# Sixteen places later for the first expert's transposes in attention's order of steps

## The chip, the cores and the metric

The kernel runs on one core of one Trainium2 chip. The metric is the device time of one execution in microseconds. An attention layer is followed by two mixture-of-experts layers, all in one launch.

## The reference

```python
def _attn_ref(q, k, v):                    # (4, 12, 448, 64), float32
    scores = (1 / sqrt(64)) * q @ k.T      # per batch and head, 448 x 448
    attn = softmax(causal(scores))
    return attn @ v

def _moe_ref(x, modality_id, w_gate, modality_bias, w1, w2):   # x: 1792 tokens x 768
    logits = x @ w_gate + modality_bias[modality_id]           # 8 experts
    e_idx = np.argmax(logits, axis=1)
    gate_w = softmax(logits)[token, e_idx]
    for e in range(8):
        h = np.maximum(x[mask] @ w1[e], 0.0)                   # 768 -> 1024
        out[mask] = gate_w[mask, None] * (h @ w2[e])           # 1024 -> 768

def reference(q, k, v, ...):
    x = attn_out.transpose(0, 2, 1, 3).reshape(1792, 768)
    return _moe2_ref(_moe_ref(x, ...), ...)                    # two such layers, the second without a bias
```

## The kernel before, in words

**Attention** works on 24 pairs of heads, numbered 0 to 23 (4 batches of 6). The work on a pair is cut into some fifty small steps, named in `ORDER`: `trans` (transposes of q and k on TensorE), `thi` and `tlo` (their high parts on ScalarE, their low parts on VectorE), `mv` (copies inside the on-chip memory, issued on SP), `score` (TensorE, L165 and L166), `mini` (mask and minimum on VectorE, L171), `expo` (ScalarE, L178, writes P), `ptrans` (TensorE, L194), `phi` and `plo` (ScalarE L201, VectorE L207), `pv` (TensorE, L214 and L215), `ocopy` (ScalarE, L220), `ria` (GpSimd, L224), `ri` (VectorE, L227), `final` (TensorE, L235), `norm` (VectorE, L244 and L246) and `store` (issued on SP, L251). A number behind the name is the head of the pair and the row block. `ORDER` is written out by hand and is run once per body; its colon number says how many pairs behind the body a step works. The text writes `norm_0@20` for that step on pair 20. Every engine, and SP, takes its instructions in the order in which the program lists them. The score banks are three, taken in turn: one of attention's own and the two banks (h0, h1) that the first expert's matmuls use later.

**Other work is hung into that order.** `ORDER` holds 24 entries `step` in each body. At each of them one entry of a list `todo` is run, and at every fifth one entry of a list `slow`. After a batch of pairs is stored, `batch` (b = 0 to 2) fills `todo` with the routing of that batch. For b = 2 the list ends with work on the **first block of the first expert** of the first expert layer, the block with which that layer begins: a gather of 128 token rows from memory into `xg` (L795, issued on GpSimd), then `XW` empty entries (`r1.wait`), then for each half g of the rows the transposes `xput` (three on TensorE, L806, into `m1xt`), `xhigh` (ScalarE, L809, into `xh`) and `xlow` (VectorE, L813, into `xl`), and last four loads that bring that expert's w2 into `raw` (L754, issued on SP, 768 KB each). `slow` brings w1 and splits it: its high parts are `high` (ScalarE, L765, some 1.05 us each), the first three low parts run on GpSimd (L769).

When no score step is left and `slow` and `todo` are both empty, each `step` runs one entry of a third list, `drain`: the first matmuls of that expert's block, `up0`, two matmuls for each of 12 pairs of column half and slice (L832 and L833, from `xh`, `xl` and the high part of w1). What is left after the last body runs behind it. Then `block0` (L851 among others) finishes the block; its second product reads w2 straight from `raw`.

```python
fs += [r1.wait, lambda: m1.gather(r1.slo[:, ds(e0["dve"] * MB, 1)], x1[: (B - 1) * S, :])] + [r1.wait] * XW
for g in range(2):
    fs += [r1.opens(lambda g=g: xput(g)), lambda g=g: m1.xhigh(t[g], g), r1.closes(lambda g=g: m1.xlow(t[g], g))]
fs += [lambda i=i: e0["second"][i]() for i in range(KF // 2)]
...
if at > free and drain and not hooks["slow"] and not todo:
    drain.pop(0)()
```

An entry marked `opens` takes a bank of the two that `trans` and `final` also use; `room` lets it run only if no more than two are held until the entry marked `closes`.

Of the kernel before, what the change touches and what calls it, by code (L numbers as in the profile page):

```python
# [324 lines left out]
            f()  # L325


PW, PL, XW = 12, 4, 8
HA, HB = 5, 5
WS, FILL = 8, 10  # L330
ET = mybir.EngineType
# [1111 lines left out]
```

## Time and profile before

| | |
|---|---|
| median of 3 runs | 960.15 us (960.14 to 960.53) |
| the profiled execution | 961.24 us |
| its span, first to last instruction | 959.3 us |
| TensorE busy in it | 913.3 us (95%) |
| VectorE, ScalarE, GpSimd busy | 627.3, 494.3, 170.8 us |
| mean granted TensorE clock | 0.984 |

The span is what the trace shows; the profiled execution is 1.94 us longer than it, and 1.09 us above the median of the runs. Times in the rows below count from the span's start, in microseconds. Attention takes the first 272 us or so, and the change stands at its end.

### The profile page before, as it was taken

The page shows a single profiled execution, that of the slowest core. Times are in us where ns is not written, and L with a number is a line of the kernel's source. Part 1 is how long each engine was busy: PE and PEld are TensorE (multiplying, and loading weights), DVE is VectorE, ACT ScalarE, POOL GpSimd, SP SyncE. Part 2 cuts the span into 40 slices and gives each one's busy share as a digit, 9 for nine tenths or more (in the row PEclk, how much of TensorE's full clock was granted, in tenths as well). Part 3 has the DMA queues.
Part 4 walks back from the last instruction along what each step waited for, and adds up shares of the span by engine and source line. Part 5 has one row for each costly group of instructions (what it writes and reads, how often), then busy time and mean ns, then how long its engine had stood idle before and what let it go on. Part 6 is the DMA issues. An engine that isn't in the chain of part 4 may idle for free. (4 is left out here: it accounts for less than half of the span.)

```text
span 959.3 us, 21195 instructions
## 1 busy us (share of the span) xinstructions
PE 913.3 (95%) x5432; PEld 808.9 (84%) x5433; DVE 627.3 (65%) x1792; ACT 494.3 (52%) x1137; POOL 170.8 (18%) x225
## 2 busy tenths in 40 slices
PE   8999999996999999997999899999999999999996
PEld 5998898986877889887898788689888888988895
DVE  4999999997574776798766778521177117383743
ACT  4998888886652222262222167322276227483653
POOL 5122414227320000000000000110112102131202
PEclk7999999999999999998999999999999999999999
DMA  6777887877249211137121135351159116395610
GB/s 124 170 185 174 185 204 186 178 165 195 95 138 343 82 49 54 64 127 251 49 66 49 45 115 200 134 212 42 40 183 357 77 46 217 105 352 221 240 49 8
DMA packets 121721, 138.50 MB, mean 144 GB/s; under 512 B 77175, under 2 KB 96759, under 8 KB 121350
## 3 DMA queue, kind: packets, MB, share of 16 engines
q1 hardware_dynamic: 116902, 118.23, 40.5%
q0 software_dynamic: 4768, 19.67, 6.0%
q8 instruction: 22, 0.36, 0.2%
q14 instruction: 29, 0.24, 0.1%
HBM read 117.69 MB, written 24.01 MB: 148 GB/s over the span
## 5 line engine op out<-in xcount | busy, mean ns | idle before, releaser
L769 DVE TENSOR_TENSOR l<-raw,h 128x768 fp32r<-128x768 f32 (+1 forms) x148 | 147.5, 1059 | 13.0 <-ACT h L765 12.7
L765 ACT CAST h<-raw 128x768 fp32r<-128x768 f32 (+1 forms) x154 | 131.3, 926 | 7.7 <-issue 5.7
L866 DVE SCALAR_TENSOR_TENSOR htl<-m2ht,hth 128x512 fp32r<-128x512 f32 x36 | 24.8, 689 | 142.7 <-ACT hth L865 142.7
L1253 DVE CUSTOM_DVE_ANT_0 junk<-y,wgb 128x768 bf16<-128x768 f32 x104 | 99.5, 956 | 14.2 <-ACTq L900 8.6
L178 ACT ACTIVATE P<-ps,m 112x336 f32<-112x336 f32 (+1 forms) x192 | 95.6, 508 | 20.5 <-DVE m L171 19.8
L844 PE MATMUL m2y<-h,hth 128*128 128x384 f32 x272 | 93.1, 342 | 0.0
L171 DVE CUSTOM_DVE_ANT_0 ps<-ps,mask 112x336 f32<-112x336 f32 (+1 forms) x192 | 85.5, 454 | 11.3 <-PE ps L163 4.6
L844 PE MATMUL m2y<-h,htl 128*128 128x384 f32 x272 | 91.5, 337 | 0.0
L832 PE MATMUL m2h<-h,xh 128*128 128x512 f32 x204 | 81.9, 401 | 1.2 <-ACTq L947 1.2
L207 DVE TENSOR_TENSOR ptl<-pp,pth 112x448 fp32r<-112x448 f32 x144 | 77.6, 539 | 8.2 <-ACT pth L201 8.1
L833 PE MATMUL m2h<-h,xl 128*128 128x512 f32 x204 | 80.9, 397 | 0.0
L194 PE MATMUL pp<-cident,P 112*112 112x112 f32 x480 | 72.5, 265 | 5.0 <-DVE ptl L207 4.5
L201 ACT CAST pth<-pp 112x448 fp32r<-112x448 f32 x144 | 67.2, 481 | 17.4 <-PE pp L194 16.7
L844 PE MATMUL m1y<-h,htl 128*128 128x384 f32 x192 | 65.9, 343 | 5.3 <-DVE htl L866 5.3
L844 PE MATMUL m1y<-h,hth 128*128 128x384 f32 x192 | 67.7, 353 | 0.0
L194 PEld LDWEIGHTS pp<-cident,P 112*112 112x112 f32 x480 | 52.8, 136 | 14.6 <-PE ps L166 5.0
L795 POOL DMA_INDIRECT xg<-y_scratch,ic x21 | 21.4, 1020 | 232.9 <-PE m2y L844 148.3
L214 PE MATMUL po<-pth,vs 112*128 112x448 f32 x192 | 62.4, 338 | 0.0
L165 PE MATMUL ps<-xk,xq 128*112 128x336 f32 (+3 forms) x184 | 61.0, 339 | 1.4 <-DMA xq<-ql 0.7
L844 PE MATMUL m2y<-l,hth 128*128 128x384 f32 x272 | 60.2, 342 | 1.1 <-issue 0.4
L795 POOL DMA_INDIRECT xg<-x_scratch,ic x16 | 16.4, 1026 | 248.3 <-PE m1y L844 223.2
L1189 POOL DMA_INDIRECT out_dram<-y,ic x19 | 36.4, 1918 | 124.2 <-ACTq L900 66.0
(459 smaller groups left out, 2202.7 us busy)
## 6 DMA issues: line engine op xcount, KB each, us to landing
raw<-in_moe_w_dram SPq DMA_DIRECT2D x46, 1536.0 KB, 10.3
xk<-xk SPq DMA_DIRECT2D x69, 112.0 KB, 3.5
y_scratch<-y SPq DMA_DIRECT2D x16, 384.0 KB
lk<-in_k_dram SPq DMA_DIRECT2D x48, 112.0 KB, 2.7
lq<-in_q_dram SPq DMA_DIRECT2D x48, 112.0 KB, 3.0
lv<-in_v_dram SPq DMA_DIRECT2D x24, 224.0 KB, 4.5
x_scratch<-xs SPq DMA_DIRECT2D x24, 224.0 KB, 3.2
xq<-ql SPq DMA_DIRECT2D x46, 112.0 KB, 3.0
```

Of the source, the lines that this page charges most:

```text
L171: nc.vector.tensor_tensor_reduce(out=s["ps", i], in0=s["ps", i], in1=mask[:, S - (i + 1) * CP :], scale=1.0, scalar=3.0e38, op0=ALU.add, o ...
L178: nc.scalar.activation(P, s["ps", i], AF.Exp, bias=s["m"][:, i : i + 1], scale=-1.0, accum_out=rs[:, j, i : i + 1])
L194: nc.tensor.transpose(pt[:, at : at + CP], s["P", i][:, kc * CP : (kc + 1) * CP], ident[:CP, :CP])
L201: nc.scalar.copy(h[:, a : a + w], pt)
L207: nc.vector.tensor_tensor(out=l[:, a : a + w], in0=pt, in1=s["pth"][:, a : a + w], op=ALU.subtract)
L214: nc.tensor.matmul(o[:, kc * CP :], vs[:, j, kc, :], s["pth"][:, seg], start=kc == 0, stop=False)
L765: self.nc.scalar.copy(hi[k], raw[:, k, :])
L769: eng.tensor_tensor(out=lo[k], in0=raw[:, k, :], in1=hi[k], op=ALU.subtract)
L832: mm(ph, xh[:, s], W.h1[k][:, f], start=k == 0, stop=False)
L833: mm(ph, xl[:, s], W.h1[k][:, f], start=False, stop=False)
L844: mm(py[n], rows[p[0]][:, s], (W.h2 if p[1] == "h" else W.l2)[k][:, f], start=k == 0 and p == "hh", stop=stop and k == ks[-1] and p == par ...
L1253: vec.tensor_tensor_reduce(out=junk, in0=y, in1=wgb[:, e], scale=1.0, scalar=0.0, op0=ALU.mult, op1=ALU.add, accum_out=r2.lg[:, e : e + 1])
```

## The change

```diff
-PW, PL, XW = 12, 4, 8
+PW, PL, XW = 12, 4, 24
```

`XW` is used in one place, the list quoted above. Between the gather and the first `xput` stand 24 empty entries instead of 8. The two groups of `xput`, `xhigh` and `xlow` and the four loads of w2, ten entries in all, move 16 entries `step` later; the gather stays. No instruction is added or taken away.

Counted along `ORDER` (the entries `step` are numbered through from the first body): the gather stands at step 641 in both. The ten entries stand at steps 650 to 659 before and 666 to 675 after. `drain` starts at step 681 in both, because the last score step lies between 680 and 681.

## Rows read from the trace of the kernel before

**Rows 1.** Page, part 1: TensorE's busy time, share and instructions (the other engines follow).
```profile
PE 913.3 (95%) x5432; PEld 808.9 (84%) x5433; DVE 627.3 (65%) x1792; ACT 494.3 (52%) x1137; POOL 170.8 (18%) x225
```
**Rows 2.** Windows: stretch, length, busy PE PEld DVE ACT POOL, clock, DMA share, GB/s.
```profile
232.95:238.72 5.77, 0.00 (x0) 0.00 (x0) 1.83 (x8) 1.40 (x6) 5.11 (x5) 0.80 0.90 293
238.72:243.30 4.58, 4.54 (x24) 4.51 (x25) 1.38 (x4) 1.35 (x4) 0.00 (x0) 0.51 1.03 366
243.30:247.70 4.40, 4.23 (x29) 3.43 (x27) 2.75 (x11) 4.12 (x10) 0.00 (x0) 1.00 0.55 174
247.70:252.00 4.30, 2.99 (x24) 2.62 (x25) 3.24 (x12) 4.30 (x14) 2.13 (x3) 1.00 0.02 4
252.00:255.00 3.00, 3.00 (x27) 2.77 (x26) 2.89 (x11) 2.98 (x11) 0.00 (x0) 1.00 0.01 3
255.00:260.00 5.00, 5.00 (x28) 4.20 (x28) 1.82 (x6) 1.74 (x5) 1.25 (x2) 1.00 0.18 46
```
**Rows 3.** Waits of PE, 229 to 275: total us, times, longest.
```profile
PE m1xt L806 <- DMA xg<-x_scratch,ic: 5.8, 1, 5.8
```
**Rows 4.** Timeline at the gather: start, length, engine, line, operation, [idle before <-releaser].
```profile
232.35 1.28 POOL L795 DMA_INDIRECT xg<-x_scratch,ic  x1 [0.19 <-DVE ql L119]
...
232.77 1.08 SPq L754 DMA_DIRECT2D raw<-in_moe_w_dram  x2
...
238.75 0.87 PE L806 MATMUL m1xt<-cident,xg 128*128 128x128 f32 x3 [5.81 <-DMA xg<-x_scratch,ic]
```
**Rows 5.** Tile xg, 225 to 245, issue to landing; the page's median of 16 such gathers.
```profile
DMA to landing us min/median/max: 6.3/6.3/6.3
...
xg<-x_scratch,ic POOLq DMA_INDIRECT x16, 3.9
```
**Rows 6.** Timeline, ScalarE from the second xhigh on, and the first up0.
```profile
243.59 0.48 ACT L809 CAST xh<-m1xt 128x384 fp32r<-128x384 f32 x1 [1.26 <-PE m1xt L806]
...
251.29 0.28 ACT L178 ACTIVATION_READ_ACCUMULATOR P<-ps,m 112x1 f32 x1
...
252.41 0.45 ACT L178 ACTIVATE P<-ps,m 112x112 f32<-112x112 f32 x1
...
254.60 0.20 ACT L178 ACTIVATION_READ_ACCUMULATOR P<-ps,m 112x1 f32 x1
...
254.86 0.19 PEld L832 LDWEIGHTS m1h0a<-h,xh 128*128 128x128 f32 x1 [0.18 <-ACT P L178]
```
**Rows 7.** Timeline, VectorE: the first xlow, then plo_1_0@22 and the end of mini_0_0@23.
```profile
241.92 0.56 DVE L813 TENSOR_TENSOR xl<-m1xt,xh 128x384 fp32r<-128x384 f32 x1 [7.08 <-ACT xh L809]
...
250.83 0.62 DVE L207 TENSOR_TENSOR ptl<-pp,pth 112x448 fp32r<-112x448 f32 x1 [0.61 <-ACT pth L201]
...
251.56 0.14 DVE L171 DVE_READ_ACCUMULATOR2_ANT m<- 112x1 f32 x1
```
**Rows 8.** Timeline: ria@21 on GpSimd, and ri@21, which reads it, on VectorE.
```profile
238.00 0.24 POOL L224 TENSOR_SCALAR ri<-rs 112x8 f32<-112x8 f32 x1
...
244.87 0.19 DVE L227 RECIPROCAL ri<-ri 112x8 f32<-112x8 f32 x1
```
**Rows 9.** Timeline, SP: store@20, then store@22 and store@23 (merged, the last at 271.69).
```profile
243.79 0.34 SPq L251 DMA_DIRECT2D x_scratch<-xs  x1
...
266.45 5.24 SPq L251 DMA_DIRECT2D x_scratch<-xs  x2
```
**Rows 10.** Windows: the first stretch of 2 us without w2's transfer.
```profile
246.00:248.00 2.00, 1.66 (x10) 1.25 (x9) 0.63 (x3) 2.00 (x5) 0.24 (x1) 1.00 0.00 1
```
**Rows 11.** Timeline, TensorE: the first readers of w2's first and second half.
```profile
274.70 2.85 PE L851 MATMUL m1y0a<-raw,wgb 128*128 128x384 f32 x8
...
280.36 2.80 PE L851 MATMUL m1y0a<-raw,wgb 128*128 128x384 f32 x8
```
**Rows 12.** Timeline, TensorE: two up0 matmuls of one kind, one entry of drain apart.
```profile
256.29 0.39 PE L832 MATMUL m1h0a<-h,xh 128*128 128x512 f32 x1
...
256.76 0.39 PE L832 MATMUL m1h0a<-h,xh 128*128 128x512 f32 x1
```

## The prediction

> **What bounds the kernel now.** I first read the busy shares: TensorE is busy for 95% of the span [rows 1], so time comes back only where TensorE stands still or runs slowly. Then I read the waits of TensorE over the end of attention. One stands far above the rest: 5.8 us at the first `xput`, which waits for the gather of the token rows [rows 3]. The timeline shows why. GpSimd issues the gather at 232.35. TensorE has emptied its queue by 232.95 and stands before the transposes until 238.75 [rows 2, 4]. The gather takes 6.3 us from issue to landing [rows 5], and the loads of w2 go out on SP 0.4 us after it [rows 4], so both transfers share the DMA engines. In the table of stretches the reader should see three things [rows 2]: no TensorE work at all in 232.95 to 238.72; a granted clock of 0.51 in the 4.58 us behind that wait, which is the lower level of 1.2 GHz, and 1.00 (2.4 GHz) afterwards; and, from 243.30 to 255, ScalarE busy for 11.40 of 11.70 us, while TensorE drops to 2.99 of 4.30 us in the middle. From 255 on TensorE is busy all the time and the others are not. So there are three limits one behind the other: a DMA wait, then ScalarE, then TensorE.
>
> **What the change moves.** Nothing is added or removed. Ten entries go from steps 650 to 659 to steps 666 to 675: six transposes, two `xhigh`, two `xlow`, four issues of w2 on SP. The second `xput` now comes just ahead of the step `expo_1_1@23`, whose work ends at 251.57 today [rows 6]. Less the 7.9 us worked out below that is about 243.7, 11 us behind the gather's issue at 232.35; the first `xput` stands some 2 us ahead of it (an estimate: three steps at about 0.6 us). Both are later than the 6.3 us of the landing, so the gather is there.
>
> The stall itself: 5.8 us of waiting goes, and 4.54 us of TensorE work at half clock becomes about 2.3 us. Ceiling: 5.8 + 2.3 = 8.1 us. At the new place I find no TensorE wait of more than about 1 us in today's trace, and there the clock is 1.00 [rows 2], so I give the clock no new loss.
>
> What is late next: I add up the busy time of each engine over the five stretches from 232.95 to 255 [rows 2], since all of that work remains to be done. ScalarE: 1.40 + 1.35 + 4.12 + 4.30 + 2.98 = 14.15 us. VectorE: 1.83 + 1.38 + 2.75 + 3.24 + 2.89 = 12.09. TensorE, with the slow stretch halved: 2.27 + 4.23 + 2.99 + 3.00 = 12.5. So of 22.05 us no more than 22.05 - 14.15 = **7.9 us** can come back, because ScalarE has its work to do, the two moved `xhigh` (0.48 each) among it.
>
> What ScalarE loses beside that. The TensorE-bound tail begins with the first `up0`. It takes score bank h0, and it waits until ScalarE has read the scores of `expo_0_2@23`, which ends at 254.80 [rows 6]. The end of this `expo` decides the gain. Two frictions are before it:
> - About 0.2 us early on, where ScalarE waits for one `mini` and for one `ptrans` that TensorE can do only after 232.95 (an estimate from the order of the steps).
> - The second moved group. `xlow` of g = 1 now stands ahead of `plo_1_0@22` and `mini_0_0@23` in VectorE's queue, and it needs the `xhigh` that stands behind `expo_1_1@23` on ScalarE. On today's axis that `expo` ends at 251.57 [rows 6]; with the first `xhigh` ahead (about 0.4) it is 251.98, and the second `xhigh` ends at 252.46. VectorE then does `xlow` 0.56, `plo` 0.62 and the `mini` of 112 columns, about 0.41 [rows 7]: 254.05. ScalarE is ready for `expo_0_0@23` at today's 252.41 plus two `xhigh` of about 0.43 each, 253.27 [rows 6]. It waits 0.8 us. Today VectorE starts that `plo` at 250.83 and ends the `mini` at 251.70, 0.7 us ahead of ScalarE [rows 6, 7], so the slack was there and is used up.
>
> Sum: 7.9 - 0.2 - 0.8 = 6.9; I take **6.8 us** for the little that such handovers add. Its ends: 7.9 with no friction (8.1, the ceiling, if the busy sum hides overlap on ScalarE), and 4.8 if both groups show their whole chain, twice transposes 0.5 + `xhigh` 0.48 + `xlow` 0.56 = 3.1 us off 7.9. The value lies nearer to the upper end because the first group meets VectorE before it has anything that ScalarE waits for.
>
> GpSimd's queue: between the gather and `ria@21` it runs one low part of w1 and `splitv`, and `ria@21` ends at 238.24 whatever TensorE does [rows 8]. Today VectorE comes to `ri@21` at 244.87, long after. In the new order it would come there at about 237.0 (244.87 less the 7.9), so it waits some 1.2 us. Behind it stands `mini_1_3@22`, and ScalarE has two slices of w1 and two `phi` to do meanwhile, so I cost this at nothing; if that cover is gone it is 1.2 us.
>
> SP's queue: the four issues of w2 pass `mv_k_3@23`, `mv_q_3@23` and `store@20`, and come to stand right behind `store@20`, ahead of `store@21`. `store@20` waits for `norm_0@20`; it goes out at 243.79 today [rows 9], and about 7.5 us sooner, at some 236.3, once the stall is gone. So w2 starts at about 237 to 239 instead of 232.8. Today its transfer runs from 232.77 to before 246 [rows 4, 10], 13.2 us at most; then it ends by about 252. Its first reader stands at 274.70, about 267.9 on the new axis [rows 11]. Cover: 16 us. Cost nothing. The `mv` copies get the DMA engines to themselves for these 4 us, which I count as nothing too, since no score step waits for them.
>
> The Trainium skill, "DMA: Bandwidth & Descriptors", section "Rules for kernel authors", speaks against this half of the change: a transfer that is to lie beside computing should be issued early and waited for late. Here the issue becomes some 4 us later; by the rows the 16 us of cover pay for that, and by the rule it would count only if the cover were gone, which is the last rival below.
>
> The drain: the last of the ten entries runs at step 675, six before `drain` starts at 681, so `up0` keeps its place and only its `xh` and `xl` come later; they are there by step 671.
>
> **The number.** The profiled execution takes 961.24 us; less 6.8 it is 954.4. It lies 1.09 us above the median of the runs, so for the median I predict 960.15 - 6.8 = **953.3 us**, 0.7% less. A measurement of this kernel can tell about 0.2% (1.9 us) from no change.
>
> **The rivals.**
> - *Half of it is given back in the tight stretch.* Both groups show their chain (4.8 us are left), and the wait at `ri@21` isn't covered either (1.2): gain 3.6, **956.5 us**. For it: ScalarE is busy 4.30 of 4.30 us exactly where the groups go [rows 2]. Against it: VectorE is busy only 3.24 of these.
> - *The change doesn't do what it says, because the list runs too long.* If `room` refuses the banks for six steps or more, or the count is off, `drain` starts late and `up0` falls behind attention. Its 12 entries take 0.47 us each [rows 12], 5.6 in all, and would no longer fill the gaps of the tail: gain 6.8 - 5.6 = 1.2, **959.0 us**, no difference. Against it: at steps 666 and 669 no `trans` is left and the next `final` comes at 672, so a bank is free.
> - *Slower: w2 comes too late.* SP is in order, and w2 now stands behind a store. If SP held it until the last store, 271.69 - 6.8 = 264.9 [rows 9], its first half would land 6.6 us later at 271.5, against a need at 267.9: 3.6 us of waiting (13.2 us for the whole, so 6.6 for a half); the second half, at 278.1 against 273.6 + 3.6 = 277.2, adds 0.9 [rows 11]. TensorE would then run at the low clock, as behind today's stall, 2.3 us: 6.8 together, no gain. The gather of the next block falls beside this transfer and would take today's 6.3 us instead of the median 3.9 [rows 5]: 2.4 more, and the kernel ends slower, at **962.6 us**. The point from which it decides is a landing of the first half some 4 us behind 268; the plan's order puts it at about 246 (237 to 239 and half a transfer).
>
> **How the numbers follow.** Forecast (gain 4.8 to 8.1, 952.0 to 955.4) 0.72; half given back 0.14; list too long 0.07; w2 late 0.05; 0.02 for no reason that I can name, as no change. The range holds forecast and first rival, from 951.9 (ceiling and 0.1 of scatter) to 956.6. Faster by over 0.2% (below 958.2): 0.72 + 0.14 + some of the third case, 0.87. Within 0.2%: 0.08. Slower by over 0.2% (above 962.1): 0.05.
>
> **What would show it.** In the changed kernel's waits of TensorE the 5.8 us line at `m1xt` is gone or under 0.5 us, and no stretch between 232 and 262 is at a clock under 0.9. The first `up0` starts at about 248.0 instead of 254.86, and everything behind it is earlier by the same amount. VectorE waits at `ri` for GpSimd near 238.2. ScalarE waits for `mini_0_0@23` for some 0.8 us. SP issues w2 between 236 and 240, and the first L851 waits for nothing. I am wrong if the stall comes up again elsewhere (at L851, or at a `final` that waits for a bank), or if the first `up0` is earlier but the end isn't.

## The result and the profile after

| | before | after |
|---|---|---|
| median of the runs beside each other | 960.33 us (4 runs, 960.14 to 960.53) | 953.03 us (4 runs, 951.76 to 953.51) |
| ratio, 95% interval | | 0.9918 (0.9891 to 0.9944) |
| beside the runs further down | 961.63 us (23 runs) | 953.97 us (6 runs), 0.9917 (0.989 to 0.9945) |
| profiled execution, its span | 961.24, 959.3 us | 953.22, 950.1 us |

The kernel became 7.3 us faster, against 6.8 forecast. The span fell by 9.2 us, more than the median; the first lines show why. They are the two timelines' twelve warm-up matmuls at the start of the program, of before and then of after, both long ahead of the change:

```profile
1.50 5.30 PE L267 MATMUL warm<-mask 112*128 112x512 bf16 x12 [1.50 <-DVE mask L259]
```

```profile
1.50 4.45 PE L267 MATMUL warm<-mask 112*128 112x512 bf16 x12 [1.50 <-DVE mask L259]
```

The same instructions take 0.85 us less, and by the gather's issue the execution after is 1.86 us ahead (230.49 against 232.35). None of this is the change, which stands behind the gather: in the traces of the runs below that have the same work ahead of the gather, its issue lies between 230.5 and 233.2. So I compare distances from the gather's issue. Timeline of after, the end of attention (columns as in [rows 4]):

```profile
230.49 1.28 POOL L795 DMA_INDIRECT xg<-x_scratch,ic  x1 [0.17 <-issue]
...
231.46 0.55 SPq L139 DMA_DIRECT2D xq<-ql  x1
...
234.29 0.32 SPq L251 DMA_DIRECT2D x_scratch<-xs  x1
...
234.81 3.16 SPq L754 DMA_DIRECT2D raw<-in_moe_w_dram  x4
...
236.47 0.20 DVE L227 RECIPROCAL ri<-ri 112x8 f32<-112x8 f32 x1 [1.82 <-POOL ri L224]
...
237.01 0.49 PE L806 MATMUL m1xt<-cident,xg 128*128 128x128 f32 x3
...
243.28 0.35 ACT L178 ACTIVATE P<-ps,m 112x112 f32<-112x112 f32 x1 [0.34 <-DVE m L171]
...
245.91 0.19 PEld L832 LDWEIGHTS m1h0a<-h,xh 128*128 128x128 f32 x1 [0.45 <-ACT P L178]
```

From the gather's issue to the first `up0` it is 15.4 us; before it was 22.5 (254.86 - 232.35, [rows 4, 6]). That is 7.1 us. The transposes come 6.5 us behind the gather's issue and wait for nothing. From there on nothing is gained or lost: from the first `up0` to the first matmul of the next block, `m1h0f`, it is 33.3 us in both, and from that to the end of the span 671.1 and 670.9. Windows of after (columns as in [rows 2]):

```profile
232.00:236.00 4.00, 3.99 (x33) 3.52 (x32) 2.60 (x9) 3.90 (x13) 3.92 (x3) 1.00 0.82 205
236.00:240.00 4.00, 2.94 (x21) 2.31 (x21) 2.68 (x11) 4.00 (x10) 2.48 (x5) 1.00 1.00 322
240.00:244.00 4.00, 3.50 (x31) 3.06 (x29) 3.25 (x10) 3.64 (x13) 0.00 (x0) 1.00 1.02 407
244.00:248.00 4.00, 3.94 (x26) 3.22 (x26) 3.19 (x13) 2.55 (x8) 0.00 (x0) 1.00 0.41 131
```

The clock stays at its upper level (2.4 GHz) throughout, and ScalarE is full, 3.90 and 4.00 of 4.00 us, just where TensorE drops to 2.94.

### The profile page after: what moved, and what is told of

Read it like the earlier page. It is cut to its first block, busy times and chain, and to the rows that moved or that the text cites. A ratio compares the mean times of both kernels' runs of the same rounds, so it can differ in the third digit from the quotient of the medians.

```text
span 950.1 us, 21195 instructions
## 1 busy us (share of the span) xinstructions
PE 907.9 (96%) x5432; PEld 804.2 (85%) x5433; DVE 626.6 (66%) x1792; ACT 494.1 (52%) x1137; POOL 170.5 (18%) x225
## 5 line engine op out<-in xcount | busy, mean ns | idle before, releaser
L832 PE MATMUL m2h<-h,xh 128*128 128x512 f32 x204 | 81.9, 402 | 1.2 <-ACTq L947 1.2
```

The costliest lines, as they stand in the source:

```text
L832: mm(ph, xh[:, s], W.h1[k][:, f], start=k == 0, stop=False)
```

## The experiments

All start from the changed kernel. Single executions of one kernel spread by several us (958.7 to 966.2 for 23 runs of the kernel before), so beside the median stands the distance in the profiled execution from the gather's issue to the first matmul of the next block (L832 on `m1h0f`). It leaves the start-up's scatter out, but it comes from one execution of each kernel. A median is read against the runs of the kernel before that stand beside it, so medians of different rows are best compared by their ratios.

| | median us | ratio to before (95%) | TensorE's longest wait there, us | gather to next block, us |
|---|---|---|---|---|
| before | 960.6 to 961.6 | | 5.8, gather | 55.9 |
| after | 953.97 | 0.9917 (0.989 to 0.9945) | 0.9 | 48.8 |
| transposes alone later | 963.51 | 1.0016 (0.9999 to 1.0032) | 6.0, copy of q | 55.1 |
| w2 alone later | 961.21 | 0.9991 (0.997 to 1.0012) | 4.7, gather | 54.7 |
| w2 right behind the copies | 955.2 | 0.9933 (0.991 to 0.9957) | 0.9 | 49.1 |
| copy from ScalarE's queue | 959.49 | 0.998 (0.9965 to 0.9995) | 3.4, copy of q | 52.7 |
| 8 places instead of 16 | 953.67 | 0.9931 (0.9916 to 0.9947) | 1.0, gather | 48.6 |
| 4 places | 957.17 | 0.9971 (0.9956 to 0.9986) | 2.7, gather | 51.1 |
| two casts on GpSimd | 953.51 | 0.9911 (0.9882 to 0.9941) | 0.9 | 47.9 |
| one cast more on ScalarE | 955.25 | 0.9943 (0.9921 to 0.9966) | 1.4 | 52.6 |
| casts of w1 sooner | 954.59 | 0.9924 (0.9906 to 0.9942) | 0.8 | 50.0 (the gather's own place in GpSimd's queue changes here) |
| list too long | 955.73 | 0.9947 (0.9927 to 0.9967) | 1.2 | 51.0 |

**The changed kernel again.**

> The changed kernel once more, beside the three that follow. Measured before: 953.0 us. Theory 1 (the gather's wait and the half clock behind it were the whole loss, and ScalarE's work takes their place): the time from the gather's issue to the first up0 matmul is 15.4 us against 22.5 in the kernel before, in every profile, and the whole is 952.5 to 953.5. Theory 2 (a part of the gain is the start-up, whose clock differs from run to run): over more runs the gain shrinks to under 6 us, 954.5 or more.

Measured: 953.97 us, 15.41 us from the gather's issue to the first `up0`. The median lies between the two ranges, but beside 23 runs of the kernel before the gain is 7.7 us and not under 6, and the way to the first `up0` is the 15.4 us of theory 1. So theory 1 holds, and the start-up doesn't make the gain.

**One half of the change: the transposes alone.**

```diff
-... + [r1.wait] * XW
+... + [r1.wait] * 14
+fs += [lambda i=i: e0["second"][i]() for i in range(KF // 2)]     # w2, at its old steps 656 to 659
+fs += [r1.wait] * 6
 for g in range(2):                                                # steps 666 to 671
     fs += [r1.opens(...), ...]
-fs += [lambda i=i: e0["second"][i]() for i in range(KF // 2)]
```

> Only the transposes stand 16 places later; w2 is issued at its old place, 0.4 us behind the gather. Theory 1: the gather takes 6.3 us again, but the transposes come 6.5 us behind its issue, so TensorE waits 0 to 0.3 us: 953.0 to 953.5. Theory 3 (moving w2 out of the way of the gather and of the copies of q and k is what pays): the gather and the copies land late beside w2, TensorE waits 2 to 4 us at the transposes or at a score, 955 to 957.

Measured: 963.51 us. The whole gain is gone, more than any of my theories said; theory 3 has the mechanism, at a price too low. Its waits of TensorE and its timeline:

```profile
PE ps L165 <- DMA xq<-ql: 6.0, 1, 6.0
```

```profile
232.87 1.08 SPq L754 DMA_DIRECT2D raw<-in_moe_w_dram  x2
234.07 0.58 SPq L139 DMA_DIRECT2D xk<-xk  x1
235.19 0.96 SPq L754 DMA_DIRECT2D raw<-in_moe_w_dram  x2
236.20 0.48 SPq L139 DMA_DIRECT2D xq<-ql  x1
...
246.81 0.68 PE L165 MATMUL ps<-xk,xq 128*112 128x448 f32 x1 [5.96 <-DMA xq<-ql]
```

The gather's wait is gone from the list. In its place TensorE stands at `score_0_3@23`, the next step that reads something SP has fetched late: the last copy of q's low part (`mv_q_3@23`). It is issued behind all four loads of w2 and lands some 10.6 us later (up to the start of the score that waits for it, 246.81 - 236.20); the tile's view shows 2.1 us for the copy of that kind that goes out at 232.22, ahead of w2:

```profile
DMA to landing us min/median/max: 2.1/2.1/2.1
```

The price is the same as at the gather, wait and cold clock:

```profile
241.00:246.00 5.00, 0.00 (x0) 0.00 (x0) 0.68 (x2) 2.44 (x9) 0.40 (x2) 0.79 0.92 320
246.00:250.00 4.00, 3.19 (x15) 3.08 (x16) 1.26 (x4) 0.81 (x2) 0.00 (x0) 0.50 0.01 5
```

The profiled execution is the fastest of the twelve, 959.9 us at a mean granted clock of 0.985; most of the others show 0.976 to 0.981. So the 55.1 us in the table are probably the low end of what this order costs, and no trace shows where the others lose the rest.

In the kernel before SP issued this copy at 236.05, just as far behind w2, and nobody met it: TensorE stood at the gather until 238.75, went on at half clock, and came to that score only at 248.7. Timeline of before:

```profile
236.05 0.50 SPq L139 DMA_DIRECT2D xq<-ql  x1
...
248.74 0.43 PE L165 MATMUL ps<-xk,xq 128*112 128x448 f32 x1
```

**The other half: w2 alone.**

```diff
-... + [r1.wait] * XW
+... + [r1.wait] * 8
 for g in range(2):                                                # the old steps 650 to 655
     fs += [r1.opens(...), ...]
+fs += [r1.wait] * 16
 fs += [lambda i=i: e0["second"][i]() for i in range(KF // 2)]
```

> Only w2 is issued 16 places later; the transposes stand where they stood. Theory 1: the gather lands after 3.9 us instead of 6.3, the wait of TensorE falls from 5.8 to 3.4 us, and the time by 2.4 us to 957.9; if the clock also stays at its upper level over the shorter wait, by 4.7 us to 955.6. Theory 3: most of the 7 us come back, 953 to 954.5. If the gather's landing doesn't depend on w2: 960.3.

Measured: 961.21 us, no difference that the interval can tell from before. Tile `xg` and the waits of TensorE:

```profile
DMA to landing us min/median/max: 5.2/5.2/5.2
```

```profile
PE m1xt L806 <- DMA xg<-x_scratch,ic: 4.7, 1, 4.7
```

The gather gains 1.1 us when w2 is out of its way, not the 2.4 I had said: this gather takes 5.1 to 5.4 us in every trace in which no load of w2 goes out in the first 4 us behind it, the page's median of 3.9 holds for others. So neither half is worth anything by itself that the medians can tell (0.8 and 1.2 us on the way to the next block), and both together are worth 7 us.

**What of w2's move counts.**

```diff
-... + [r1.wait] * XW
+... + [r1.wait] * 19
+fs += [lambda i=i: e0["second"][i]() for i in range(KF // 2)]     # steps 661 to 664
+fs += [r1.wait]
 for g in range(2):                                                # steps 666 to 671
```

> The run in which w2 stays at its old place waits 6.0 us at a score, for the copy of q's low part that SP issued right behind w2. Here the transposes stand 16 places later, and w2's four issues stand at steps 661 to 664: right behind that last copy in SP's queue, some 2.5 us sooner than in the changed kernel and still beside the gather. Theory 4 (what matters of w2's move is that it passes the last copies of q and k; anything further is worth nothing): no wait at the score, 953 to 954.5. Theory 5 (w2 must start late, whatever it passes): the copies or the gather are late, TensorE waits 2 us or more, 956 to 962.

Measured: 955.2 us, and 49.1 us to the next block, 0.3 more than the changed kernel; TensorE's list has no wait for a copy. SP's timeline:

```profile
232.74 0.55 SPq L139 DMA_DIRECT2D xq<-ql  x1
233.50 2.06 SPq L754 DMA_DIRECT2D raw<-in_moe_w_dram  x3
```

The median lies between the two ranges; the waits decide, and by them theory 4 holds: w2 has only to stand behind the last copy, 0.8 us is enough. The 2.5 us more that the change gives it are worth nothing that these runs can show.

**Queue or engines.** In the run with the transposes alone later, the one copy goes out from ScalarE's queue:

```diff
-nc.sync.dma_start(to.bitcast(F32), src.bitcast(F32))
+eng = nc.scalar if (n, nm, step) == (npair - 1, "q", 3) else nc.sync
+eng.dma_start(to.bitcast(F32), src.bitcast(F32))
```

> As the run in which the transposes alone stand later and w2 at its old place, but the one copy for which TensorE waited there (q's low part of the last pair) is issued from ScalarE's queue instead of SP's. Theory 6 (the copy is late because it stands behind w2 in one queue): it lands 2 to 4 us after its issue, TensorE waits under 1 us, 953.5 to 955. Theory 7 (it is late because the DMA engines are full of w2, whichever queue it is in): it lands 8 to 10 us after its issue, the wait of some 5 us stays, 961 to 964.

Timeline (the line numbers are one higher in this kernel):

```profile
232.09 1.08 SPq L755 DMA_DIRECT2D raw<-in_moe_w_dram  x2
...
235.95 0.54 ACTq L140 DMA_DIRECT2D xq<-ql  x1
...
243.44 0.69 PE L166 MATMUL ps<-xk,xq 128*112 128x448 f32 x1 [3.35 <-DMA xq<-ql]
```

Measured: 959.49 us; the copy lands 7.5 us behind its issue instead of 10.6, and the wait is 3.4 instead of 6.0. That lies between the two theories, and both have a part. Windows of this run:

```profile
242.00:244.00 2.00, 0.56 (x2) 0.52 (x3) 0.05 (x1) 0.67 (x4) 0.00 (x0) 0.50 1.03 361
244.00:246.00 2.00, 2.00 (x12) 1.93 (x10) 0.69 (x2) 0.45 (x1) 0.00 (x0) 0.50 0.62 207
```

From a queue of its own the copy lands while the DMA engines are still busy with w2 (1.03 in the window of 243.44); in SP's queue the score started only at 246.81, when they had all but run empty (0.01 from 246 to 250). The place behind w2 in one queue costs some 3 us: 3.1 counted from the copy's issue, 2.6 counted from w2's first (246.81 - 232.87 against 243.44 - 232.09). The other 5.4 us (7.5 against 2.1) remain in a queue of its own, beside engines whose mean busy share is 1.00 to 1.07 in the windows from 236 to 242. The Trainium skill, "DMA: Bandwidth & Descriptors", "Issuing engines are not separate DMA queues", says that transfers of all issuing engines run on the same 16 engines and interleave; the 7.5 us agree with it.

**How many places it needs.**

```diff
-PW, PL, XW = 12, 4, 24
+PW, PL, XW = 12, 4, 16      # and 12
```

> XW = 16: the ten entries stand 8 places later than before instead of 16, the first transposes at step 658, w2 at 664 to 667, behind the store of pair 20. Theory 1: TensorE comes to the transposes about 4.5 us behind the gather's issue, the gather without w2 beside it lands after 3.9 us, so there is no wait: 952.5 to 953.5, as with 16 places. Rival (the gather needs its 6.3 us also without w2): a wait of some 2 us, 955.

> XW = 12: four places later, the first transposes at step 654, w2 at 660 to 663, now right before the store of pair 20 in SP's queue but behind all copies of q and k. Theory 1: TensorE comes to the transposes some 2.3 us behind the gather's issue and waits 1.6 us if the gather takes 3.9 us, 4 us if w2 is beside it again: 955 to 957, between the kernel before and the one with eight places. Rival (a matter of 16 places, not of the landing): 959 to 960.3.

Waits of TensorE, eight places, then four:

```profile
PE m1xt L806 <- DMA xg<-x_scratch,ic: 1.0, 1, 1.0
```

```profile
PE m1xt L806 <- DMA xg<-x_scratch,ic: 2.7, 1, 2.7
```

With 0, 4, 8 and 16 places the wait is 5.8, 2.7, 1.0 and 0 us, and the way to the next block 55.9, 51.1, 48.6 and 48.8. The wait of 1.0 us at eight places, between theory 1's none and the rival's 2, costs nothing that the way to the next block shows. At four places one load of w2 is again ahead of the copy of q, against what I had expected; the gather lands after 5.7 us there, and the copy costs no wait. The windows show the clock at 0.70 behind the 2.7 us and at 1.00 behind the 1.0 us:

```profile
236.00:240.00 4.00, 3.00 (x16) 2.82 (x17) 1.88 (x6) 1.76 (x4) 0.97 (x2) 0.70 1.03 361
```

```profile
236.00:240.00 4.00, 3.65 (x27) 3.23 (x28) 3.25 (x13) 3.47 (x8) 1.59 (x4) 1.00 0.96 287
```

(four places first). So the matter is the landing, 5.1 us behind the issue (5.7 at four places), and eight places would have done as far as these runs can tell.

**What bounds the stretch now.**

```diff
-slow.append(lambda k=k: W.high(1, k))
+slow.append(lambda k=k: W.high(1, k) if k < 4 else nc.gpsimd.tensor_copy(W.h1[k], W.raw1[:, k, :]))
```

> The changed kernel, but the casts of w1's slices 4 and 5 to their high parts run on GpSimd instead of ScalarE. Theory 1 (ScalarE bounds the stretch behind the gather): ScalarE is rid of two casts of 0.93 us, the first up0 comes up to 1.9 us sooner, 951.1 to 952.2. Rival (VectorE's queue with the moved xlow and the late ri bounds it): no more than 0.4 us, 952.6 to 953.0.

```diff
 slow.append(lambda k=k: W.high(1, k))
+if k == KD - 1:
+    slow.append(lambda k=k: W.high(1, k))
```

> The changed kernel with one cast of w1's slice 5 done twice on ScalarE, five steps behind the first. Theory 1 (ScalarE bounds the stretch): plus 0.9 us, 953.9. Rival (VectorE or TensorE bounds it, ScalarE has room): no change, 953.0.

Two casts off ScalarE give 0.9 us in the trace (47.9 against 48.8), of 1.9 that they take; the median, 953.51 against 953.97, can't tell it from the changed kernel. Timeline of that run:

```profile
238.25 0.20 DVE L227 RECIPROCAL ri<-ri 112x8 f32<-112x8 f32 x1 [1.83 <-POOL ri L224]
...
239.06 0.63 ACT L178 ACTIVATE P<-ps,m 112x448 f32<-112x448 f32 x1 [0.92 <-DVE m L171]
```

So ScalarE bounds the stretch, and the next limit stands 1 us behind it: with the cast of slice 4 gone, ScalarE comes too early to `expo_1_3@22` and waits 0.92 us for the `mini` that stands behind `ri@21` on VectorE, which still waits for GpSimd. This is the cover that the prediction named for `ri@21`.

One cast more costs 3.8 us in the trace, where 0.9 was expected; by the ratios (0.9943 against 0.9917) it is 2.5 us, within their intervals. Timeline and windows of that run:

```profile
244.42 0.35 ACT L178 ACTIVATE P<-ps,m 112x112 f32<-112x112 f32 x1 [0.34 <-DVE m L171]
```

```profile
243.00:244.00 1.00, 0.00 (x0) 0.00 (x0) 0.95 (x2) 1.00 (x4) 0.00 (x0) 1.00 1.03 415
244.00:245.00 1.00, 0.71 (x6) 0.74 (x6) 1.00 (x6) 0.53 (x3) 0.00 (x0) 0.75 0.92 365
245.00:246.00 1.00, 1.00 (x8) 1.00 (x7) 1.00 (x6) 0.84 (x2) 0.00 (x0) 0.50 0.21 83
...
250.00:251.00 1.00, 1.00 (x6) 0.90 (x5) 0.00 (x0) 0.28 (x1) 0.00 (x0) 0.50 0.00 0
```

Up to `expo_0_0@23`, the first of these lines, the price can be read by itself: it starts 13.7 us behind the gather's issue (244.42 - 230.71) against 12.8 in the changed kernel (243.28 - 230.49). That is the 0.9 us of theory 1, so ScalarE's work is on the path. At the same time TensorE's wait for the `plo` behind that work grew to 1.4 us, and the clock went to its lower level (1.2 GHz) until about 251; the other 2.9 us fall into that stretch.

> The changed kernel with the casts of w1 to its high parts 5 to 15 steps sooner on ScalarE (steps 625 to 650) and the three low parts on GpSimd later (steps 660 to 670). The gather is then not behind a low part on GpSimd, and ria of pair 21 neither. Theory 1 (ScalarE and the late ri limit the stretch behind the gather): the first up0 comes 1 to 2 us sooner, 951.5 to 952.5. Rival (the stretch before is as full, 4.4 of 5 us of ScalarE, and takes the casts' time): within 0.5 us of the changed kernel.

```diff
-for k in range(KD):
-    slow.append(lambda k=k: W.high(1, k))
-    if k < EARLY:
-        slow.append(lambda k=k: W.low(1, k, nc.gpsimd))
+slow.extend([lambda k=k: W.high(1, k) for k in range(KD)] + [r1.wait])
+slow.extend([lambda k=k: W.low(1, k, nc.gpsimd) for k in range(EARLY)])
```

Measured: 954.59 us, ratio 0.9924 (0.9906 to 0.9942). That is the changed kernel's time within what can be told, and not the gain of theory 1. The gather is issued from GpSimd without the low part ahead of it, but what ScalarE is spared behind the gather it has to do ahead of it (busy 9.01 us from 220 to 230, against 8.60 in the changed kernel). That fits the rival.

**The list too long.**

```diff
-PW, PL, XW = 12, 4, 24
+PW, PL, XW = 12, 4, 40
```

> XW = 40: the ten entries stand at steps 682 to 691, so drain starts at 692 instead of 681, and w2 behind the store of pair 21. It measures the rival of the prediction in which the list runs too long. By that rival's price (12 entries of 0.47 us that no longer fill gaps) up to 5.6 us of the gain are lost, 958.6. Theory 1 (the tail is bound by TensorE's own work, and what fills it later is done anyway): a loss of 0 to 2 us, 953 to 955. w2 is issued at about 246 and lands before 259, ahead of its reader at 265.

Measured: 955.73 us, between theory 1's 955 and the rival's 958.6, and 2.2 us more on the way to the next block. `drain` starts 11 steps later and the first `up0` 20.4 us behind the gather's issue instead of 15.4, yet from there to the next block it is 30.6 us instead of 33.3. So most of the rival's 5.6 us isn't lost. Here too the clock was low, in a stretch whose longest wait of TensorE was 1.2 us:

```profile
240.00:244.00 4.00, 2.69 (x16) 2.33 (x17) 3.32 (x13) 4.00 (x13) 2.12 (x3) 0.81 0.00 0
244.00:248.00 4.00, 4.00 (x21) 3.82 (x20) 2.21 (x9) 1.70 (x7) 0.00 (x0) 0.50 0.00 2
```

## Why the prediction was right, and where it wasn't

**The stall and what takes its place: right.** 5.8 us of wait and the half clock behind it went, ScalarE became the limit, and 7.1 us came back on the way to the first `up0`, of 7.9 that ScalarE's work allowed; 6.8 were forecast. With the start-up's 1.86 us taken off, the first `up0` lies at 247.8 on the old axis, where 248.0 was said.

**The frictions: right in kind.** VectorE waits 1.82 us at `ri` for GpSimd (1.2 said). ScalarE behind it isn't late, by a narrow margin: the run with two casts on GpSimd shows the cover gone. ScalarE waits 0.34 us for `mini_0_0@23` (0.8 said). The sum of the frictions, 1.0, came out at 0.8.

**The gather's landing: too short in one place.** I used 6.3 us beside w2, which holds (6.0 again with w2 there), and in the last rival 3.9 us without it; here it is 5.1 to 5.4. The places of the transposes were too late: I had the second `xput` 11 us behind the issue and the first some 2 us ahead of it, and they came 9.4 and 6.5 us behind. I had taken the time from ScalarE's `expo`, and TensorE runs ahead of ScalarE there. The conclusion, that they come later than the landing, stands, at 6.5 against 5.1; against the 6.3 that I used only 0.2 us would have been left.

**w2: the step that failed.** I costed its move at nothing, with 16 us of cover ahead of its reader, and wrote of the `mv` copies that have the DMA engines to themselves for these 4 us that they count "as nothing too, since no score step waits for them". The cover holds: the first reader, L851, waits for nothing. The copies don't count as nothing. `score_0_3@23` waits for one of them as soon as the gather's wait is gone, 6.0 us if w2 is ahead of it. w2's move is half of the gain in the sense that without it there is none. The total came out right because the change moves both, which in this term is luck: the working would have forecast 953.3 for the transposes alone, where 963.5 was measured. What I read past was SP's order: w2 goes out at 232.77 [rows 4], and the last copies stand behind it in the same queue. I asked who waits for a copy today; the question was who would come to it next with the stall gone.

**The Trainium skill's rule** ("DMA: Bandwidth & Descriptors", "Rules for kernel authors": issue a DMA early, wait late) I had set against 4 us less of cover. The trace goes further: here the early issue itself does the harm, 55.1 us against 49.1 to the next block between w2 ahead of the last copy and right behind it. The rule holds for the one transfer, and says nothing of the small ones queued behind it.

**The rivals.** Half given back: no, 0.8 us of 7.9. List too long: not the case, and its price when brought about is 2.2 us in the trace, in which the clock fell too, not 5.6. w2 late: no; L851 doesn't wait.

## What to carry to other kernels

- A long wait hides other late things. Before a wait is taken away, list what the engine comes to next and when each of those lands, by each DMA queue's order; the next late one takes the wait's place, as the copy of q did at 6.0 us.
- A large load that nobody needs soon belongs behind the small copies that somebody needs soon, not ahead of them; a queue of its own helps only in part (10.6 us became 7.5, against 2.1 without the load).
- Moving a consumer later by hand need only reach the landing: eight places gave all that sixteen did, as far as these runs can tell.

## What the runs showed of the hardware that I had not expected

- A copy of 112 KB inside the chip took 10.6 us behind 3 MB of loads in the same queue, 7.5 us from another queue beside them, and 2.1 us without them.
- The clock fell to 0.50 in two runs in which TensorE's longest single wait was 1.2 and 1.4 us, and stayed at 1.00 in the changed kernel, where it was 0.9 us. I had counted the clock as safe there. What decides it, these runs don't settle.
- The same start-up took 0.85 us more or less for its first twelve matmuls from one execution to the next, and the gather's issue at some 231 us moved by up to 2.7 us between traces.
